# Issuing the second MLP product of a step two steps late instead of one, in a fused attention, MoE and DFT kernel

## The chip, the cores and the metric

The kernel runs as one program on one core of a Trainium2 chip. The metric is the time of one execution in device microseconds. Lower is better; the runs of one kernel are summed up by their median.

## The reference, cut to what matters

Three parts follow one another. Shapes: batch B = 4, 768 tokens, model width 384 (8 heads of 48), hidden width 1536.

```
# 1. attention with a complex decay, a recurrence over the tokens
for t in range(S):
    S = a[t] * S + k[t] v[t]^T        # a complex, S a 48 x 48 state for each head
    y[t] = q[t] @ real(S)
# 2. first MoE: tokens mixed through rank 32, then an MLP
u = x + (x^T @ U @ V)^T
x = u + relu(u @ w_ch1) @ w_ch2       # 384 -> 1536 -> 384
# 3. second MoE: 2-D Fourier transform over tokens and channels, norm, MLP
u = x + real(fft2(x))
n = (u - mean) / sqrt(var + 1e-6)
out = u + relu(n @ w_ch1) @ w_ch2
```

## The kernel before, in words

Precision. Values are kept as pairs of a high and a low part, and a product of two pairs is three matmuls (`mm3`, L89 to L93: high by high, high by low, low by high), each of 128x128 by 128x384.

The MLP, the part that the change touches. Both MoEs run through `moe_units`. The work is a row of 96 steps (b, g, f) for each MoE: batch b, half g of its tokens (384), block f of 128 hidden units out of 12. A step is

- the first product: three `mm3`, nine matmuls, into the PSUM bank `hp`;
- `hh`, the high part of relu(hp), by ScalarE (L182), and `hl`, the low part, by VectorE from `hp` and `hh` (L184); both are traced with high priority;
- the second product `second()`: nine matmuls that add the step's share to three PSUM banks `acc` (three token blocks of 128). Six of them take `hh` (L91, L92), three take `hl` (L93). At f = 11 the group (b, g) is finished: VectorE adds `acc` to `x` (L661) and SP stores it, in the second MoE to the output.

In a step the code calls the second product of the step before: the list `late` holds one step. `hp` has two PSUM banks (pool `phid`), `acc` three, everything else that needs PSUM shares three (`pms`). `hh` and `hl` have the pool's default of two buffers each.

Work beside it. While the first MoE of batch b runs, the attention of batch b+1 is traced between its steps by a `Side` object, which meters it out at an even rate: decays and their logarithms (`L`, `s`, `Th`), queries and keys (`QK`, stored and loaded again transposed as `QT`), scores `sc` with their mask `pm`, values split in two parts (`vh`, `vl`, from the loaded `vin`), the products `y` and `g` and the state `S`. Beside the last batch's first MoE and beside the second MoE it is the DFT of a batch (`f`, `ee`, `oo`, `P`, `Q`, `p_`, the normalised rows `un`). Beside the first group of the program and around the border of the two MoEs the weights are also unpacked from float64 words (`stw`, `wxw`, `w`).

Order. All of this is traced in one program order with priorities; a scheduler then gives each engine a fixed list, and an engine carries out its list in order. An instruction that has to wait holds up what stands behind it on the same engine. SP's list holds most loads and stores, and a load that waits for its buffer holds up the loads behind it. Tiles come from pools: a tile of a tag is written only when the last reader of the tile that had the buffer before is done.

Of the kernel before, what the change touches and what calls it, by code (L numbers as in the profile page):

```python
# [29 lines left out]
GSCALE = 2.0**-10  # L30
YSCALE = 2.0**-10 / FSCALE
RE_MID = 0.9
RE_LEAST = 0.72
# [8 lines left out]
def mixer_kernel(ctx, tc, a_in, qk_in, v_in, u_in, v4_in, w_in, cc_in, ss_in, cb_in, sb_in, id_in, mask_in, rows_in, out):  # L42
# [56 lines left out]
    def anchor():  # L99
        """What is kept comes after what was traced so far, on its engine."""  # L100
        for i in nc.cur_bb.bb.instructions:
            anchors[i.engine] = i
# [9 lines left out]
    def from_f64(src, name, signs=False):  # L112
        """
        Reads float64 words (as pairs of int32) and makes float32 of their bits. The high word,
        taken as a float32, is scaled by 2^-112: that takes 896 off its float64 exponent.
        """
        n = src.shape[-1]
        st = moe.tile([128, 384, 2], I32, tag="u", name=f"st{name}", bufs=5)[:, :n]
        nc.sync.dma_start(st.rearrange("p n w -> p (n w)"), src.bitcast(I32))
        low, high = st[:, :, 0], st[:, :, 1]  # L120
        x = slot(f"wx{name}")[:, :n]
        xi = x.bitcast(I32)
        kept(A.activation, x, high.bitcast(F32), AF.Abs, scale=2.0**-112)
        kept(V.tensor_scalar, low, low, 29, None, ALU.logical_shift_right)
        V.scalar_tensor_tensor(out=xi, in0=xi, scalar=3, in1=low, op0=ALU.logical_shift_left, op1=ALU.bitwise_or)  # L125
        if signs:
            A.activation(high.bitcast(F32), high.bitcast(F32), AF.Sign)
            G.tensor_tensor(x, x, high.bitcast(F32), ALU.mult)
        else:
            V.scalar_tensor_tensor(out=xi, in0=high, scalar=-(2**31), in1=xi, op0=ALU.bitwise_and, op1=ALU.bitwise_or)  # L130
        return x
# [17 lines left out]

    # ------------------------------------------------------------------ MoE  # L150
    def moe_units(mi, uT, finish, extra, batches=range(B)):
        """Hidden steps (b, g, f); the output products of a step come one step later."""
        acc = {}
# [16 lines left out]
        for b in batches:  # L170
            for g in range(2):
                for f in range(FB):
                    w = wt[mi, f]
                    hp = phid.tile([128, 512], F32, tag="hid", name=f"hp{mi}_{b}_{g}_{f}")[:, :384]
                    for k in range(3):
                        u = uT(b, g)[k]
                        ks = slice(k * 128, (k + 1) * 128)
                        mm3(hp, (w[:, 0, ks], w[:, 1, ks]), (u[:, 0], u[:, 1]), k == 0, k == 2)
                    yield b, g, f, 0
                    with tc.high_priority():  # L180
                        hh = moe.tile([128, 384], F32R, tag="hh", name=f"hh{mi}_{b}_{g}_{f}")
                        A.activation(hh, hp, AF.Relu)  # L182
                        hl = moe.tile([128, 384], F32R, tag="hl", name=f"hl{mi}_{b}_{g}_{f}")
                        V.scalar_tensor_tensor(out=hl, in0=hp, scalar=0.0, in1=f32(hh), op0=ALU.max, op1=ALU.subtract)  # L184
                    yield b, g, f, 1
                    for args in late:
                        second(*args)
                    late = [(b, g, f, hh, hl)]
        second(*late[0])

    # ------------------------------------------------------------------ attention
    BOUNDS = {
# [26 lines left out]
    def load(kind, m):  # L219
        """Decays, or queries and keys, of a pair of chunks."""  # L220
        if m >= len(PAIRS):
# [10 lines left out]
    def load_vs():  # L232
        """All values of the first batch."""
        for c0, c1 in ((0, 4), (4, NC)):
# [5 lines left out]
    def load_v(b, c):  # L240
        if c == NC:
            b, c = b + 1, 0
        if 0 < b < B:
            t = attention_pool()(f"vin{b}_{c}", "vin", 2, (128, DM))
            nc.sync.dma_start(t, v_in[b, c])
            inp["v", b, c] = t
# [6 lines left out]
    def parts(m):  # L253
        """The first pair goes chunk by chunk, so that its products start early."""
        return [slice(0, 1), slice(1, 2)] if m == 0 else [slice(0, 2)]

    def decays(m):
        """Decayed queries and keys of a pair of chunks and the tangents of its turns."""
        b, cc = PAIRS[m]
# [28 lines left out]
        def steady(js):  # L288
            """Counts re >= RE_LEAST + im^2 / 4: then |im / re| stays under 1.2."""
            re, s2_, th = of(js, a[:, 0], s2, Th)  # L290
# [4 lines left out]
        def least_re(js):  # L295
            """The same of the first batch, in two parts."""
            (re,) = of(js, a[:, 0])
            V.tensor_scalar(unread(js), re, RE_LEAST, 0.0, ALU.is_ge, ALU.add, accum_out=stat("re", b, cc[js.start]))
# [66 lines left out]
    def turns(m):  # L365
        """Rotates the queries and keys of a pair of chunks."""
        b, cc = PAIRS[m]
# [48 lines left out]
    def products(m, j):  # L416
        """Scores, outputs and the next state of one chunk."""
        b, cc = PAIRS[m]
# [44 lines left out]
        def summed(out, rows, ops):  # L463
            """Sums over the products of pairs, head by head, in plain float32 or of float16 parts."""
            for o, (l, r) in enumerate(ops):
# [73 lines left out]
        if not last:  # L539
# [13 lines left out]
            else:  # L553
# [3 lines left out]
                summed(gp, 128, [(hs(kh), vh), (hs(kh), vl), (hs(kl), vh)])  # L557
        x = xt[b, c] = xpl[0].tile([128, DM], F32, tag="x", name=f"x{n}", bufs=10)
        A.activation(x, yp, AF.Copy, scale=1.0 / FSCALE if plain else YSCALE)
# [12 lines left out]

    # ------------------------------------------------------------------ first MoE
    zst = {}
# [12 lines left out]
    def prelim(b):  # L587
        """The low-rank mixing of the tokens: z = U^T x, kept as a stack of parts."""
        zp = bank(f"z{b}", phid if b == 0 else pms)[:, :DM]
# [19 lines left out]
    def make_ut(b, g):  # L609
        """u^T = x^T + (U V part)^T of 384 tokens, as three (hi, lo) pairs."""  # L610
        uts[b, g] = pieces = []
        xs = {}

        def turn(k):
# [3 lines left out]
            if (b, g) == (0, 0):  # L618
                xs[k] = xpl[0].tile([128, DM], F32, tag="x", name=f"xs0_0_{k}", bufs=10)
            else:  # L620
# [58 lines left out]
    def urgent(gen, n=None):  # L679
        """Steps that go before what was traced up to n instructions ago."""  # L680
        while True:
# [77 lines left out]
    class Side:  # L759
        """Steps that go between the MoE's: `total` steps over `slots` slots."""  # L760

# [12 lines left out]

    # ------------------------------------------------------------------ 2-D DFT, norm, second MoE
    pfl = [None]
# [16 lines left out]
    def dft(b):  # L793
        """u = x + Re(DFT2(x)); rows 384 + j of u hold token 768 - j (j > 0) and 384 (j = 0)."""
        (cch, ccl), (ssh, ssl), (cbh, cbl), (sbh, sbl) = (fc[x] for x in ("cc", "ss", "cb", "sb"))
# [13 lines left out]
        def fold(out, x, op):  # L809
            """Columns d and 384 - d."""  # L810
            n = 193 if op == ALU.add else 192
# [48 lines left out]
        for j in range(3):  # L860
            js = slice(j * 128, (j + 1) * 128)
            pp = bank(f"P{b}_{j}")[:, :194]
            for m, w in enumerate((128, 66)):
                mm3(pp, (ach[:w, m, js], acl[:w, m, js]), (cbh[:w, m], cbl[:w, m]), m == 0, m == 1)
            p_ = ft(f"p_.{b}_{j}", [128, 194], bufs=2)
            A.copy(p_, pp)
# [37 lines left out]
    def make_un(b, g):  # L904
        """Normalised rows, transposed, as three (hi, lo) pairs."""
        mv, rs = rstd[b]
# [21 lines left out]

    # ------------------------------------------------------------------ the program
    ident = const("ident", [128, 128])  # L930
# [76 lines left out]

    # ------------------------------------------------------------------ any other decays and sizes
    def verdict():
        """1 where a bound of the chunked attention's number range was not kept, as an int32."""  # L1010
        tests = [(i, test) for i, x in enumerate(BOUNDS.values()) for test in x]
# [11 lines left out]
    def recurrence(xd):  # L1023
        """The attention token by token; partitions (b, x quarter, h), decays of any size."""
        N = 32
# [73 lines left out]
    def rest(xd):  # L1099
        """Everything after the attention, one batch at a time."""  # L1100
        with tc.For_i(0, B, 1) as bv:
# [4 lines left out]
            for c in range(NC):  # L1106
                xt[r, c] = xpl[0].tile([128, DM], F32, tag="x", name=f"xr{c}", bufs=10)
                nc.sync.dma_start(xt[r, c], xd[bass.ds(bv, 1), c].rearrange("o p m -> (o p) m"))
# [116 lines left out]
```

## Time and profile before

| | before |
|---|---|
| median of 3 runs | 1039.2 us (1037.37 to 1039.5) |
| profiled execution, its span on the core | 1035.1 us |
| TensorE matmuls busy | 885.1 us (86% of the span) |
| TensorE weight loads busy | 841.7 us (81%) |
| VectorE busy | 690.3 us (67%) |
| ScalarE busy | 441.3 us (43%) |
| GpSimd busy | 443.3 us (43%) |

The profile gives the span of the execution that it shows, from the first to the last instruction on the core; 4.1 us lie between it and the median of the runs. An engine's busy time is the time in which it carries out an instruction. Engines are named PE (TensorE's matmuls), PEld (its weight loads), DVE (VectorE), ACT (ScalarE), POOL (GpSimd) and SP (the queue that issues transfers). Seen roughly, the first 130 us are the attention of the first batch, up to about 535 us the first MoE runs beside the attention of the other batches, up to about 697 us it runs beside the DFT of the first batches, and from there on it is the second MoE.

### The profile page before, as it was taken

The numbers are of one execution on the slowest core, as the hardware profiler recorded it, in microseconds if no ns is written. First come the engines' busy times: TensorE is split into PE (matmuls) and PEld (weight loads), VectorE is DVE, ScalarE is ACT, GpSimd is POOL, SyncE is SP. The second block draws the span as 40 slices with busy tenths as digits, with TensorE's granted clock in tenths as the row PEclk, the third lists the DMA queues.
The fourth block names the chain that finished last, engine by engine and source line by source line (L and its number), as shares of the span: only waits on it lengthen the run. The fifth ranks groups of instructions, "written<-read, shape, count | busy, mean of one in ns | idle before, by whom it ended". The sixth has DMA issues, their size and how long they took to land. (4 is left out here: it accounts for less than half of the span.)

```text
span 1035.1 us, 16471 instructions
## 1 busy us (share of the span) xinstructions
PE 885.1 (86%) x6338; PEld 841.7 (81%) x6338; DVE 690.3 (67%) x1104; ACT 441.3 (43%) x841; POOL 443.3 (43%) x426
## 2 busy tenths in 40 slices
PE   0059978788778787798899999779999999999997
PEld 0048777578777787787899999779999999999997
DVE  7997988897877689788764727886535554362121
ACT  6436565657545555555643224465212211222111
POOL 4445646575464645656446307776312222020000
PEclk9999899979898898989899999889999999999999
DMA  8078646834516152614135103342101021000000
GB/s 346 0 103 165 194 81 138 166 69 109 94 45 121 49 93 69 115 48 93 33 61 200 39 1 115 108 144 77 62 16 47 2 77 46 1 23 19 7 23 27
DMA packets 47097, 83.43 MB, mean 81 GB/s; under 512 B 5600, under 2 KB 36064, under 8 KB 47008
## 3 DMA queue, kind: packets, MB, share of 16 engines
q1 hardware_dynamic: 45152, 75.96, 30.8%
q0 software_dynamic: 1856, 6.31, 1.7%
q8 instruction: 52, 0.85, 0.4%
q14 instruction: 37, 0.30, 0.1%
HBM read 53.79 MB, written 9.44 MB: 61 GB/s over the span
## 5 line engine op out<-in xcount | busy, mean ns | idle before, releaser
L184 DVE SCALAR_TENSOR_TENSOR hl<-hp,hh 128x384 fp32r<-128x384 f32 x192 | 105.4, 551 | 191.8 <-ACT hh L182 186.6
L182 ACT ACTIVATE hh<-hp 128x384 fp32r<-128x384 f32 x192 | 93.1, 488 | 270.9 <-PE hp L93 249.1
L91 PE MATMUL acc<-w,hh 128*128 128x384 f32 x576 | 202.4, 352 | 2.0 <-ACT hh L182 2.0
L93 PE MATMUL acc<-w,hl 128*128 128x384 f32 x576 | 166.1, 352 | 38.4 <-DVE hl L184 38.2
L92 PE MATMUL acc<-w,hh 128*128 128x384 f32 x576 | 197.4, 343 | 0.0
L93 PEld LDWEIGHTS acc<-w,hl 128*128 128x128 f32 x576 | 106.9, 195 | 45.4 <-DVE hl L184 45.1
L91 PEld LDWEIGHTS acc<-w,hh 128*128 128x128 f32 x576 | 111.4, 193 | 4.3 <-ACT hh L182 3.0
L92 PEld LDWEIGHTS acc<-w,hh 128*128 128x128 f32 x576 | 111.5, 194 | 0.0
L91 PE MATMUL hp<-u,w 128*128 128x384 f32 x288 | 103.0, 359 | 6.2 <-ACT w L141 3.1
L92 PE MATMUL hp<-u,w 128*128 128x384 f32 x288 | 103.7, 360 | 1.2 <-POOL u L630 1.0
L93 PE MATMUL hp<-u,w 128*128 128x384 f32 x288 | 102.4, 356 | 0.0
L92 PE MATMUL hp<-n,w 128*128 128x384 f32 x288 | 96.9, 336 | 1.6 <-DVE n L920 1.6
L91 PE MATMUL hp<-n,w 128*128 128x384 f32 x288 | 96.5, 336 | 1.1 <-ACT n L919 1.1
L93 PE MATMUL hp<-n,w 128*128 128x384 f32 x288 | 96.8, 336 | 0.0
L437 PE MATMUL sc<-QT 96*128 96x128 f32 x384 | 66.6, 328 | 11.4 <-DMA QT<-QK 10.5
L437 PEld LDWEIGHTS sc<-QT 96*128 96x128 f32 x384 | 60.7, 232 | 14.3 <-issue 11.3
L142 POOL TENSOR_TENSOR w<-wxw,w 128x384 fp32r<-128x384 f32 x48 | 58.8, 1235 | 21.9 <-ACT w L141 21.7
L451 PE MATMUL kp<-ident,QK 128*128 128x128 f32 x120 | 20.5, 297 | 53.7 <-POOL QK L409 48.6
L91 PEld LDWEIGHTS hp<-u,w 128*128 128x128 f32 x288 | 58.5, 203 | 7.0 <-ACT w L141 3.3
L451 PEld LDWEIGHTS kp<-ident,QK 128*128 128x128 f32 x120 | 16.1, 155 | 55.5 <-POOL QK L409 48.6
L92 PEld LDWEIGHTS hp<-u,w 128*128 128x128 f32 x288 | 58.6, 203 | 2.2 <-POOL u L630 1.6
L93 PEld LDWEIGHTS hp<-u,w 128*128 128x128 f32 x288 | 58.3, 203 | 0.0
(302 smaller groups left out, 2056.4 us busy)
## 6 DMA issues: line engine op xcount, KB each, us to landing
QT<-QK SPq DMA_DIRECT2D x144, 129.0 KB
stw<-in_w_dram SPq DMA_DIRECT2D x48, 384.0 KB
ain<-in_a_dram SPq DMA_DIRECT2D x12, 768.0 KB
qkin<-in_qk_dram SPq DMA_DIRECT2D x12, 768.0 KB
x1d<-x SPq DMA_DIRECT2D x24, 192.0 KB
vin<-in_v_dram SPq DMA_DIRECT2D x18, 192.0 KB
lo<-x1d SPq DMA_DIRECT2D x12, 192.0 KB
out_dram<-lo SPq DMA_DIRECT2D x12, 192.0 KB
```

Of the source, the lines that this page charges most:

```text
L91: T.matmul(o, ah, bh, start=start, stop=False, skip_group_check=skip)
L92: T.matmul(o, ah, bl, start=False, stop=False, skip_group_check=skip)
L93: T.matmul(o, al, bh, start=False, stop=stop, skip_group_check=skip)
L142: G.tensor_tensor(w[:, 1, zs], x, f32(w[:, 0, zs]), ALU.subtract)
L182: A.activation(hh, hp, AF.Relu)
L184: V.scalar_tensor_tensor(out=hl, in0=hp, scalar=0.0, in1=f32(hh), op0=ALU.max, op1=ALU.subtract)
L437: T.matmul(ps[:, h, :], q[:, 128:256], q[:, :128], start=True, stop=True)
L451: T.transpose(kp[z][:, i * 128 : (i + 1) * 128], QK[:, z, i, 128:256], ident)
```

## The change

The second product of a step is issued two steps later: the list `late` holds two steps, and only what lies deeper is issued. So `hh` and `hl` live one step longer and get three buffers each. To make room, `vin` (loaded values) goes from two buffers to one, `x` (the attention's output, input of the MoE) from ten to nine, and `p_` (a piece of the DFT) from two to one. Line numbers after the change are one to two higher.

```diff
+LATE = 2
...
                     with tc.high_priority():
-                        hh = moe.tile([128, 384], F32R, tag="hh", name=f"hh{mi}_{b}_{g}_{f}")
+                        hh = moe.tile([128, 384], F32R, tag="hh", bufs=LATE + 1, name=f"hh{mi}_{b}_{g}_{f}")
                         A.activation(hh, hp, AF.Relu)
-                        hl = moe.tile([128, 384], F32R, tag="hl", name=f"hl{mi}_{b}_{g}_{f}")
+                        hl = moe.tile([128, 384], F32R, tag="hl", bufs=LATE + 1, name=f"hl{mi}_{b}_{g}_{f}")
                         V.scalar_tensor_tensor(out=hl, in0=hp, scalar=0.0, in1=f32(hh), op0=ALU.max, op1=ALU.subtract)
                     yield b, g, f, 1
-                    for args in late:
-                        second(*args)
-                    late = [(b, g, f, hh, hl)]
-        second(*late[0])
+                    late.append((b, g, f, hh, hl))
+                    if len(late) > LATE:
+                        second(*late.pop(0))
+        for args in late:
+            second(*args)
...
-            t = attention_pool()(f"vin{b}_{c}", "vin", 2, (128, DM))
+            t = attention_pool()(f"vin{b}_{c}", "vin", 1, (128, DM))
...
-        x = xt[b, c] = xpl[0].tile([128, DM], F32, tag="x", name=f"x{n}", bufs=10)
+        x = xt[b, c] = xpl[0].tile([128, DM], F32, tag="x", name=f"x{n}", bufs=9)
...
-            p_ = ft(f"p_.{b}_{j}", [128, 194], bufs=2)
+            p_ = ft(f"p_.{b}_{j}", [128, 194], bufs=1)
```

The first place is VectorE in the first batch's second group (b = 0, g = 1), from `hl` of step 2 on. The names end in the step and a running number (`hl_0_1_3_...` is batch 0, group 1, step 3). Before:

```order
L184 SCALAR_TENSOR_TENSOR hl_0_1_2_2048<-hp_0_1_2_2008,hh_0_1_2_2046 128x384
L442 TENSOR_TENSOR pm_5_0_2286<-sc_5_0_2242,mask 128x512
L565 SCALAR_TENSOR_TENSOR S_4_2198<-g_4_2197,S_4_2198 96x384
L313 SCALAR_TENSOR_TENSOR L_2_2630<-s_2_2631,L_2_2630 128x768
L353 SCALAR_TENSOR_TENSOR s_0_2034<-Th_0_2035,s_0_2034 128x768
L501 TENSOR_TENSOR ql_5_2291<-QT_5_1893,qh_5_2290 96x1024
L381 SCALAR_TENSOR_TENSOR Th_0_2035<-one,T_0_2032 128x256 x2
L487 SCALAR_TENSOR_TENSOR vl_0_2621<-vin_0_2315,vh_0_2620 128x384
L381 SCALAR_TENSOR_TENSOR Th_0_2035<-one,T_0_2032 128x256
L184 SCALAR_TENSOR_TENSOR hl_0_1_3_2106<-hp_0_1_3_2074,hh_0_1_3_2104 128x384
L442 TENSOR_TENSOR pm_5_1_2298<-sc_5_1_2281,mask 128x512
L184 SCALAR_TENSOR_TENSOR hl_0_1_4_2232<-hp_0_1_4_2187,hh_0_1_4_2230 128x384
```

And with the change, from just behind `pm` of the same chunk on:

```order
L567 SCALAR_TENSOR_TENSOR S_4_2189<-g_4_2188,S_4_2189 96x384
L185 SCALAR_TENSOR_TENSOR hl_0_1_3_2097<-hp_0_1_3_2065,hh_0_1_3_2095 128x384
L315 SCALAR_TENSOR_TENSOR L_2_2621<-s_2_2622,L_2_2621 128x768
L355 SCALAR_TENSOR_TENSOR s_0_2022<-Th_0_2023,s_0_2022 128x768
L503 TENSOR_TENSOR ql_5_2282<-QT_5_1884,qh_5_2281 96x1024
L383 SCALAR_TENSOR_TENSOR Th_0_2023<-one,T_0_2020 128x256 x2
L489 SCALAR_TENSOR_TENSOR vl_0_2612<-vin_0_2306,vh_0_2611 128x384
L383 SCALAR_TENSOR_TENSOR Th_0_2023<-one,T_0_2020 128x256
L444 TENSOR_TENSOR pm_5_1_2289<-sc_5_1_2272,mask 128x512
L185 SCALAR_TENSOR_TENSOR hl_0_1_4_2223<-hp_0_1_4_2178,hh_0_1_4_2221 128x384
```

Seven instructions of the attention have moved from ahead of `hl` of step 3 to behind it; ahead of `hl` of step 4 stand the same ones as before.

The second place is TensorE around the same step. Before, from the second product of step 3 (the high part) to the first product of step 5; of each run of matmuls on one tile some rows stand:

```order
L92 MATMUL acc_0_1_2_1998<-w_3_860,hh_0_1_3_2104 128x384
L599 MATMUL z_2398<-xh_0_2399,ust 128x384
L600 MATMUL z_2398<-xl_0_2400,ust 128x384
L599 MATMUL z_2398<-xh_1_2405,ust 128x384
L93 MATMUL acc_0_1_0_1996<-w_3_860,hl_0_1_3_2106 128x384
L93 MATMUL acc_0_1_1_1997<-w_3_860,hl_0_1_3_2106 128x384
L93 MATMUL acc_0_1_2_1998<-w_3_860,hl_0_1_3_2106 128x384
L91 MATMUL hp_0_1_5_2271<-u_1_0_1690,w_5_954 128x384
```

With the change, from the end of the first product of step 4 on:

```order
L94 MATMUL hp_0_1_4_2178<-u_1_2_1821,w_4_934 128x384
L92 MATMUL acc_0_1_0_2053<-w_2_770,hh_0_1_2_2034 128x384
...
L94 MATMUL acc_0_1_2_2055<-w_2_770,hl_0_1_2_2036 128x384
L439 MATMUL sc_5_1_2272<-QT_5_1884 128x128 x4
L92 MATMUL hp_0_1_5_2262<-u_1_0_1681,w_5_954 128x384
...
L94 MATMUL hp_0_1_5_2262<-u_1_2_1821,w_5_954 128x384
L92 MATMUL acc_0_1_0_2053<-w_3_860,hh_0_1_3_2095 128x384
...
L94 MATMUL acc_0_1_2_2055<-w_3_860,hl_0_1_3_2097 128x384
```

Behind the first product of step 4 now stand the second product of step 2, the first of step 5 and only then the second of step 3.

The third place is VectorE at the end of the first MoE (batch 3, group 1, steps 10 and 11; `f`, `eel`, `oo` and `un` belong to the DFT of the second batch or to the second MoE's input). Before:

```order
L184 SCALAR_TENSOR_TENSOR hl_3_1_9_6742<-hp_3_1_9_6713,hh_3_1_9_6740 128x384
L812 TENSOR_TENSOR f_1_7056<-xo_1_7052 128x191
L911 TENSOR_SCALAR un_1_1_7207<-hi_1_5821,mv_6224,rs_6420 128x384
L812 TENSOR_TENSOR f_1_7056<-ye_1_7053 128x192
L814 COPY f_1_7056<-ye_1_7053 128x1
L831 TENSOR_TENSOR ee_6972<-f_1_7056 128x193 x2
L911 TENSOR_SCALAR un_1_2_7209<-hi_2_5822,mv_6224,rs_6420 128x384
L184 SCALAR_TENSOR_TENSOR hl_3_1_10_6800<-hp_3_1_10_6770,hh_3_1_10_6798 128x384
L840 TENSOR_TENSOR eel_7118<-ee_6972,eeh_7117 128x776
L812 TENSOR_TENSOR f_1_7056<-x_1_1_7050 128x191
```

With the change, from the same `hl` on:

```order
L185 SCALAR_TENSOR_TENSOR hl_3_1_9_6733<-hp_3_1_9_6704,hh_3_1_9_6731 128x384
L109 TENSOR_SCALAR stw_5_1_6641<-stw_5_1_6641 128x384
L185 SCALAR_TENSOR_TENSOR hl_3_1_10_6791<-hp_3_1_10_6761,hh_3_1_10_6789 128x384
L126 SCALAR_TENSOR_TENSOR wxw_5_1_6643<-wxw_5_1_6643,stw_5_1_6641 128x384
L109 TENSOR_SCALAR stw_6_0_6671<-stw_6_0_6671 128x384
L126 SCALAR_TENSOR_TENSOR wxw_6_0_6673<-wxw_6_0_6673,stw_6_0_6671 128x384
L814 TENSOR_TENSOR f_0_6983<-xe_0_6978 128x192
L816 COPY f_0_6983<-xe_0_6978 128x1
L814 TENSOR_TENSOR f_0_6983<-xo_0_6979 128x191
L185 SCALAR_TENSOR_TENSOR hl_3_1_11_6842<-hp_3_1_11_6819,hh_3_1_11_6840 128x384
```

The pieces `f_1`, `ee`, `un` and `eel` of the second half have moved to behind the last `hl` of the first MoE.

## Rows read from the trace of the kernel before

**Rows 1.** Page, engines: busy us (share of the span) and instructions.
```profile
PE 885.1 (86%) x6338; PEld 841.7 (81%) x6338; DVE 690.3 (67%) x1104; ACT 441.3 (43%) x841; POOL 443.3 (43%) x426
```

**Rows 2.** Busy time by stretch (start:end, length; columns in the first row).
```profile
core 0: us, PE busy (x) PEld busy (x) DVE busy (x) ACT busy (x) POOL busy (x), PEclk, DMA share, GB/s
...
240.00:535.00 295.00, 244.43 (x1983) 233.27 (x1982) 232.33 (x300) 164.43 (x303) 163.21 (x148) 0.91 0.37 74
535.00:625.00 90.00, 88.88 (x644) 87.11 (x643) 41.11 (x74) 28.17 (x61) 31.26 (x36) 1.00 0.25 84
625.00:697.00 72.00, 61.14 (x337) 57.84 (x335) 64.41 (x118) 35.74 (x76) 54.84 (x58) 0.91 0.38 117
697.00:1035.00 338.00, 331.47 (x2001) 327.54 (x1998) 142.37 (x319) 76.21 (x161) 62.26 (x79) 0.99 0.11 34
```

**Rows 3.** Page, chain that ended last, shares by engine.
```profile
PE 32%; DVE 4%; issue 1%; DMA 1%; POOL 1%; ACT 0%; DVEq 0%; SPq 0%; POOLq 0%
```

**Rows 4.** Page, costliest groups: count, busy, mean ns, idle before and what ended it.
```profile
L93 PE MATMUL acc<-w,hl 128*128 128x384 f32 x576 | 166.1, 352 | 38.4 <-DVE hl L184 38.2
```

**Rows 5.** Waits of PE from 240 to 535: us in total, times, longest.
```profile
PE acc L93 <- DVE hl L184: 26.8, 10, 6.4
PE g L469 <- DVE kl L461: 15.1, 6, 5.4
```

**Rows 6.** Waits of DVE from 240 to 535.
```profile
DVE L L326 <- POOL s L325: 16.0, 4, 7.2
DVE hl L184 <- ACT hh L182: 11.8, 10, 3.5
DVE pm L442 <- PE sc L437: 9.2, 7, 3.1
...
DVE S L565 <- PE g L469: 2.2, 2, 1.6
```

**Rows 7.** Timeline of PE: start us, us, instruction [idle before, what ended it].
```profile
260.23 0.34 PE L599 MATMUL z<-xh,ust 128*128 128x384 f32 x1
266.98 1.33 PE L93 MATMUL acc<-w,hl 128*128 128x384 f32 x3 [6.42 <-DVE hl L184]
...
394.29 0.62 PE L93 MATMUL acc<-w,hl 128*128 128x384 f32 x2 [2.72 <-DVE hl L184]
```

**Rows 8.** Timeline of DVE from 250 to 268.
```profile
250.72 0.56 DVE L184 SCALAR_TENSOR_TENSOR hl<-hp,hh 128x384 fp32r<-128x384 f32 x1 [0.43 <-ACT hh L182]
...
262.93 2.95 DVE L487 SCALAR_TENSOR_TENSOR vl<-vin,vh 128x384 f16<-128x384 f32 x1
...
266.40 0.52 DVE L184 SCALAR_TENSOR_TENSOR hl<-hp,hh 128x384 fp32r<-128x384 f32 x1
...
267.45 0.54 DVE L184 SCALAR_TENSOR_TENSOR hl<-hp,hh 128x384 fp32r<-128x384 f32 x1
```

**Rows 9.** Busy time from 260 to 270, columns as in rows 2.
```profile
260.00:270.00 10.00, 3.58 (x13) 3.26 (x12) 10.00 (x12) 1.13 (x2) 6.69 (x4) 0.67 0.07 20
```

**Rows 10.** Timeline of PE in the second MoE.
```profile
899.94 0.33 PE L91 MATMUL hp<-n,w 128*128 128x384 f32 x1
...
901.33 0.34 PE L93 MATMUL hp<-n,w 128*128 128x384 f32 x1
```

**Rows 11.** Waits of PE from 625 to 697.
```profile
PE acc L93 <- DVE hl L184: 5.7, 3, 3.6
```

**Rows 12.** Groups of DVE instructions from 649 to 697: count, busy us, mean ns, idle before.
```profile
L812 DVE TENSOR_TENSOR f<-ye 128x192 f32<-128x192 f32 x2 | 4.7, 2334 | 0.0
```

**Rows 13.** DMA issues from 240 to 535.
```profile
vin<-in_v_dram SPq DMA_DIRECT2D x10, 192.0 KB
```

**Rows 14.** Tile `vh`: idle time before its instructions, by what ended it.
```profile
  DMA vin<-in_v_dram: 3.8, 1
```

**Rows 15.** Tile `x`: its transfers, issue to landing.
```profile
DMA to landing us min/median/max: 5.2/5.2/5.2
```

More of the change, by code (lines that the diff above doesn't have):

```diff
@@ L618, in turn @@
             if (b, g) == (0, 0):
-                xs[k] = xpl[0].tile([128, DM], F32, tag="x", name=f"xs0_0_{k}", bufs=10)
+                xs[k] = xpl[0].tile([128, DM], F32, tag="x", name=f"xs0_0_{k}", bufs=9)
             else:
@@ L1106, in rest @@
             for c in range(NC):
-                xt[r, c] = xpl[0].tile([128, DM], F32, tag="x", name=f"xr{c}", bufs=10)
+                xt[r, c] = xpl[0].tile([128, DM], F32, tag="x", name=f"xr{c}", bufs=9)
                 nc.sync.dma_start(xt[r, c], xd[bass.ds(bv, 1), c].rearrange("o p m -> (o p) m"))
```

## The prediction

> **What bounds the kernel now.** I read the page first, then the busy times by stretch, then the waits of TensorE and VectorE in the longest attention stretch, then one wait instruction by instruction. TensorE is busy for 885.1 of 1035.1 us [rows 1], and the chain that ended last is mostly its matmuls [rows 3]: any gain has to come out of the time in which it stands or runs at its lower clock. The table by stretch [rows 2] says where that is. From 697 on (second MoE) TensorE is busy for 331.47 of 338.00 us at a granted clock of 0.99, from 535 to 625 for 88.88 of 90.00: together 7.7 us are idle, with nothing worth having. From 240 to 535, where the attention of the next batch runs beside the first MoE, it is busy for 244.43 of 295.00 us, so 50.6 are idle, at a clock of 0.91; from 625 to 697 (border to the second MoE) 10.9 of 72 are idle. VectorE is busy for 232.33 of the 295 and for 64.41 of the 72, so in the second case it paces the stretch.
>
> The change can act on one kind of wait: the third matmul of each triple, on `hl`, stands for 26.8 us, in ten waits, in 240 to 535 [rows 5], of 38.4 in the whole execution [rows 4]; three more cost 5.7 us in 625 to 697 [rows 11]. The next one in the list, `g<-kl` with 15.1, is attention work that the change doesn't shorten. On VectorE's side the idle time is spread: 16.0 us on GpSimd's `s`, 11.8 on ScalarE's `hh`, 9.2 and 2.2 on TensorE's `sc` and `g` [rows 6]. Only the last two items are TensorE being late.
>
> **The change, step by step.** *No instruction is added or removed*: 18 matmuls, one `hh`, one `hl` a step as before. At the undisturbed rate nine matmuls start within eight pitches from 899.94 to 901.33 [rows 10], 0.174 us each; a step of 18 costs 3.1 us, three matmuls 0.52, twelve 2.1.
>
> *What a second step of delay buys.* Take the longest wait. TensorE finishes its last covered matmul at 260.23 + 0.34 = 260.57 and stands for 6.42 us until `hl` of step 3 is there at about 266.9 [rows 7]. VectorE had finished the `hl` before it at 251.3; nine other operations came next, `vl` with 2.95 us the longest, and only at 266.40 did this `hl` start [rows 8]. The order of the changed kernel (VectorE's rows in the section on the change) puts this `hl` ahead of seven of them, which looks like the whole 6.42. But the seven now stand between it and `hl` of step 4, which is no earlier: it ran at 267.45 to 267.99 [rows 8] behind the same work. There are two PSUM banks for `hp`, so the first product of step 6 cannot start before `hl` of step 4 has read its bank. Until then TensorE has what its rows in that section show: nine matmuls of `hp` of step 5 and the three `hl` matmuls of step 3 more than before, 2.1 us. It stands from 262.7 to 268.0, resumes 1.0 us later than before and 2.1 us further on. **This place gains 1.1 us of 6.4.** The wait is handed to the next bank, not removed.
>
> *The nine others in this stretch.* In eight of them the order likewise puts the `hl` that was waited for ahead of the work that delayed it; in the ninth (first step of a group) five more operations come ahead of it. For each of the nine waits whose `hl` moves, the least is the three matmuls by which the need for `hl` moves away in the plain pattern (15 matmuls between the end of `hp` and the first use before, 18 after): 0.52 us. The place worked out gives 1.1, and the ceiling is the whole 26.8. So 4.7 to 9.9 us, and I take the middle, **-7.3**.
>
> *What is given back at the group borders.* I gave every VectorE instruction its own duration from the trace and summed what stands ahead of each `hl` in the two orders. Inside a group the sum falls by 1 to 12 us a step; at the first step of the next group it is back: -1.2, +4.1 and 0.0 us in the three borders of this stretch. Side work is put off, not saved, and VectorE has to have done it all by then. The +4.1 falls on a step at which TensorE waited already; one more step of products (3.1) covers part of it. Between 0 and +4.1 I take **+2**.
>
> *The border to the second MoE.* Here the three waits (5.7) lose their cause, but 14.8 us of VectorE work (pieces of the next DFT: `f`, `ee`, `oo`, `un`; [rows 12] has their largest group) go from ahead of the last `hl` of the first MoE to behind it, and at the first `hl` of the second MoE the sum is +1.3. VectorE idles 7.6 of the 72 us, so that it decides here. Between -1.6 (three times 0.52) and +7 (below) I take **0**. Second MoE: more slack for a wait that isn't there, 0; its cover is the 98% of TensorE's time.
>
> *Fewer buffers.* With one buffer for `vin` the load of a chunk has to wait until `vl` of the chunk before has read it, and SP's queue behind it (loads of `QT`, of the next decays) waits too. Ten loads in 295 us [rows 13] are 29 us apart, and 192 KB land in 5.2 us, as the transfers of `x` do [rows 15], so I take 0; unhidden it costs one wait like the 3.8 us that `vh` had once [rows 14]. One `x` less makes the fourth `x` of a batch wait for a store, 5.2 us at three batch borders if ScalarE stands there with `hh` behind it; hidden by the steps between, 0. `p_` is a copy of 194 columns on a stretch with a full TensorE: 0.
>
> **Sum**: -7.3 + 2 + 0 + 0 = -5.3. The profiled execution has a span of 1035.1 us, 4.1 under the median of the runs, 1039.2; 1029.8 and the same 4.1 make **1034**. 0.2%, about 2 us, is what a measurement of this kernel can tell from no change.
>
> By the Trainium skill ("Perfetto Trace Analysis", Identifying the Most-Contended Engine) TensorE's headroom is judged by the busy share of its weight loads, not of its matmuls, and VectorE's by occupancy; by that, these two are level in 240 to 535, 233.27 and 232.33 us of 295 [rows 2], and the rule would have the change gain nothing there, since it takes no work from either. The trace agrees with the level shares; it also shows VectorE idle for 62.7 us, which leaves room for a gain, so that the rule makes a rival and not the forecast.
>
> **Rivals.** *A, the forecast*: small gain at each wait, part given back; own range 1028 to 1037; 41%. *B, VectorE paces the stretch anyway*: what TensorE gains inside a group it loses standing at the next border or at `g<-kl`. For it: the sums that return to about 0, and 16.0 us on GpSimd's `s`, that no order of `hl` shortens. Against it: 11.4 us of VectorE's idle time is TensorE's lateness. No change, 1039; 27%. *C, slower, by the border to the second MoE*: 14.8 + 1.3 = 16.1 us more VectorE work stand between the last `hl` of one MoE and the first of the other, covered by one more step, 3.1; with the 5.7 of before given back that is 16.1 - 3.1 - 5.7 = +7, and with nothing won before, 1046. It decides if VectorE does not use the earlier time, that is if its idle time in this stretch grows above 7.6 us. Against it: the work ahead of that border is only 1.3 us more, so a VectorE that never idles arrives as before. 21%. *D, the waits really go*: nine waits, 26.8 - 2.7 = 24.1 us, vanish (the tenth is the one at a group's first step [rows 7]), since TensorE's earlier `sc` and `g` also pull VectorE's chain forward (the 11.4 us); with +2 that is -22, 1017. For it: the clock, whose mean over the 10 us with the longest wait was 0.67 [rows 9], between its levels of 2.4 GHz (1.0) and 1.2 GHz (0.5), stays up too. Against it: the bank of `hp`. 11%.
>
> **Numbers.** 1034 is A. The range reaches half-way into D and C, 1024 to 1043, which leaves out about 6 and 11 in 100. Faster: nearly all of A (0.39), D, and 0.04 of B, 0.54; within 0.2%: 0.19 of B, 0.02 of A and 0.03 of C, 0.24; slower 0.22.
>
> **What the changed profile would show.** Right: `acc` on `hl` almost gone from TensorE's waits, and in its place `hp` on `hl` (the bank), two thirds as long; idle time of TensorE in the attention stretch down by some 5 of 50.6 us; the second MoE as long as before. Wrong: `hp<-hl` short as well and the attention stretch 20 us shorter (D); TensorE's idle time unchanged, with more of it right behind a group's last step (B); VectorE idle above 7.6 us and TensorE's waits above 12 us around the border to the second MoE (C); or ScalarE standing at `x` or `vh` for a DMA (the buffers).

## The result and the profile after

The changed kernel takes 1053.17 us (median of 4 runs, 1050.76 to 1053.86) against 1038.86 before: a ratio of 1.0133, 95% interval 1.0113 to 1.0152. It is slower by 14 us where 5 us of gain were forecast, and lies outside the range (1024 to 1043). The profiled executions differ by 16.9 us in span (1052.0 against 1035.1); the one of the changed kernel is the slowest of its four, so part of the 16.9, which is 2.6 more than the medians differ by, is spread between executions.

The page of the changed kernel, in the order of [rows 1] and [rows 3], with the granted clock in 40 slices between them:

```profile
PE 889.1 (85%) x6338; PEld 842.3 (80%) x6338; DVE 688.4 (65%) x1104; ACT 442.6 (42%) x841; POOL 429.9 (41%) x426
...
PEclk9978998878889898899899999959999999999999
...
PE 41%; DVE 22%; DMA 7%; ACT 5%; issue 4%; POOL 2%; SPq 1%; DVEq 0%; POOLq 0%; ACTq 0%
```

The work is the same and no engine is busier than before by more than 4 us, so most of the time went into standing. The clock has a hole (5) at two thirds of the span, at the border of the two MoEs. The shares of the two chains can't be held against each other: the chain before [rows 3] is followed back only to 633 us, the new one to 180. From the last group of the first MoE on, which both cover, VectorE has 38 us in the one and 37 in the other.

To place the loss I took the start of `hh` of the same step in ScalarE's timeline of both profiles:

| step (MoE, batch, half, f) | before, us | after, us | later by |
|---|---|---|---|
| 0, 0, 1, 0 | 239.9 | 240.8 | 0.8 |
| 0, 1, 1, 0 | 388.0 | 392.4 | 4.4 |
| 0, 2, 0, 0 | 464.1 | 467.9 | 3.8 |
| 0, 2, 1, 0 | 533.7 | 541.6 | 8.0 |
| 0, 3, 1, 0 | 627.9 | 635.1 | 7.2 |
| 0, 3, 1, 11 | 678.4 | 678.9 | 0.5 |
| 1, 0, 0, 0 | 694.9 | 708.3 | 13.5 |
| 1, 0, 1, 0 | 736.6 | 750.7 | 14.1 |
| 1, 3, 1, 11 | 1025.4 | 1040.5 | 15.1 |

Two stretches lose: the attention stretch up to step (0, 3, 1, 0) 6.4 us, and the last group of the first MoE with the border behind it, up to (1, 0, 1, 0), 6.9 us. Inside the last group 6.7 us are won, and 13.0 are lost between its last step and the next group's first. The second MoE keeps its length within 1 us. The last 1.8 us to the span's end are mostly no loss: with two steps of delay one more second product, nine matmuls or 1.6 us, is left behind the last `hh`.

**The attention stretch.** TensorE's waits in the changed kernel from 240 to 560, to be held against [rows 5]:

```profile
PE hp L92 <- DVE hl L185: 16.3, 5, 7.3
PE xp L619 <- DVE pm L444: 6.7, 3, 3.2
PE g L471 <- ACT kh L462: 6.6, 1, 6.6
PE kp L453 <- DVE pm L444: 4.2, 4, 1.8
PE z L602 <- DVE xl L600: 3.9, 1, 3.9
PE kp L453 <- DVE xs L629: 3.9, 3, 2.4
PE y L471 <- DVE pm L444: 3.6, 3, 2.3
PE g L471 <- DVE kl L463: 3.2, 2, 2.2
```

The waits of `acc` on `hl` (26.8 us) left the list; `hp` now waits for `hl` (16.3), and most of the other lines are attention and token-mixing work of TensorE waiting for VectorE. Its waits on `pm`, `xs` and `xl` rose from 2.7 us to 22.3; for some 16 of these the operation waited for stands one or two `hl` further back in VectorE's list than before, for the rest, with the longest wait on `pm` (3.2), it does not. The waits of `g` on `kl` fell from 15.1 to 3.2, and one of 6.6 on ScalarE's `kh` is new. The sum did not fall. The next fences are the busy times by group (columns as in [rows 2]), before and after, each from a group's first `hh` to the next:

```profile
239.90:316.10 76.20, 58.47 (x454) 55.46 (x453) 61.12 (x79) 41.68 (x77) 41.66 (x33) 0.92 0.35 77
316.10:388.00 71.90, 61.23 (x530) 58.85 (x530) 53.42 (x71) 42.03 (x80) 38.04 (x42) 0.89 0.44 81
388.00:464.10 76.10, 62.26 (x463) 58.29 (x462) 62.53 (x81) 41.18 (x75) 44.29 (x32) 0.89 0.33 70
464.10:533.70 69.60, 61.28 (x531) 59.47 (x530) 54.13 (x72) 38.34 (x74) 38.02 (x41) 0.93 0.37 68
```

```profile
240.80:319.00 78.20, 60.38 (x406) 56.52 (x404) 58.81 (x74) 40.87 (x75) 40.32 (x31) 0.85 0.33 73
319.00:392.40 73.40, 60.42 (x582) 57.08 (x581) 58.77 (x81) 44.52 (x82) 42.77 (x46) 0.95 0.42 93
392.40:467.90 75.50, 60.74 (x408) 57.17 (x408) 58.29 (x74) 38.98 (x71) 34.19 (x28) 0.84 0.33 71
467.90:541.60 73.70, 63.68 (x568) 60.03 (x567) 53.04 (x73) 40.24 (x74) 37.90 (x44) 0.91 0.33 60
```

TensorE is busy for 243.2 of 293.8 us before and 245.2 of 300.8 after: 50.6 us idle became 55.6, and as good as the same number of matmuls (1978 and 1964 rows) took 2.0 us more. The counts by group show that whole pieces of attention moved from one group to the next (454 to 406, then 530 to 582). VectorE does not pace this stretch by its work: it is busy for 231.2 us before and 228.9 after, so its idle time rose too, from 62.6 to 71.9.

**The border to the second MoE.** TensorE's timeline in the changed kernel, where its longest new wait is:

```profile
683.07 0.69 PE L94 MATMUL acc<-w,hl 128*128 128x384 f32 x1 [2.21 <-DVE hl L185]
...
690.21 0.52 PE L93 MATMUL hp<-n,w 128*128 128x384 f32 x1
690.53 0.52 PE L94 MATMUL hp<-n,w 128*128 128x384 f32 x1
700.95 0.53 PE L92 MATMUL ac<-cc,eeh 128*128 128x194 f32 x1 [9.90 <-ACT eeh L841]
```

And what it waited for, on VectorE and on ScalarE:

```profile
694.94 1.16 DVE L814 TENSOR_TENSOR f<-xe 128x192 f32<-128x192 f32 x1
...
699.40 0.63 DVE L833 TENSOR_TENSOR ee<-f 128x193 f32<-128x193 f32 x2
```

```profile
700.06 0.84 ACT L841 CAST eeh<-ee 128x776 fp32r<-128x776 f32 x1 [3.34 <-DVE ee L833]
...
701.66 0.47 ACT L921 CAST n<-nt 128x384 fp32r<-128x384 f32 x1
```

Most of the pieces `f` and `ee` of the DFT that stood ahead of the last `hl` now run from 682.9 on, behind it. TensorE's list has the DFT's product `ac` next, which needs them (`eeh`); and the third row block `n`, which the first products of the second MoE need, stands behind `eeh` on ScalarE. So both of TensorE's jobs wait for the same late pieces. From the last `hh` of the first MoE to the first of the second (678.39 to 694.86 before, 678.86 to 708.32 after) VectorE is nearly full in both kernels, but with 15.66 us of work before and 28.68 after:

```profile
678.39:694.86 16.47, 12.18 (x66) 11.08 (x66) 15.66 (x27) 11.43 (x25) 12.00 (x13) 0.85 0.36 115
```

```profile
678.86:708.32 29.46, 15.40 (x57) 13.14 (x58) 28.68 (x48) 12.48 (x26) 21.39 (x23) 0.56 0.30 90
```

Busy time around the wait, with the change:

```profile
680.00:682.00 2.00, 0.86 (x5) 0.54 (x4) 2.00 (x4) 0.85 (x3) 2.00 (x2) 1.00 0.00 0
684.00:690.00 6.00, 4.57 (x14) 3.55 (x13) 5.85 (x13) 1.92 (x4) 3.84 (x5) 0.50 0.43 132
690.00:700.00 10.00, 1.05 (x4) 0.54 (x2) 9.89 (x19) 1.39 (x3) 7.28 (x7) 0.50 0.46 138
700.00:710.00 10.00, 9.05 (x41) 8.64 (x41) 9.48 (x15) 7.70 (x16) 5.97 (x8) 0.50 0.20 45
714.00:716.00 2.00, 2.00 (x14) 2.00 (x13) 1.65 (x4) 1.85 (x4) 0.98 (x2) 1.00 0.13 12
```

TensorE is idle and VectorE full for 10 us. The granted clock is 1.00 up to 682 and 0.50 from 684 on, TensorE's lower level of 1.2 GHz: it fell ahead of the long wait, where TensorE had been busy for 0.86 of 2.00 us and stood for 2.21 us on `hl`. It stays at 0.50 through the wait and the 10 us after it, and is back at 1.00 in 714 to 716. Two matmuls of 128x384 start 0.32 us apart there (690.21 and 690.53) and 0.174 in [rows 10]. From 680 to 716 the mean granted clock is 0.57, and 0.91 in the same stretch of the kernel before. The Trainium skill ("TensorE: Matmul & The Clock Gate", "What's actually happening") says that an idle TensorE is clocked at 1.2 GHz; the trace agrees, with 0.50 from 690 to 700, where TensorE is busy for 1.05 us.

### The profile page after: what moved, and what is told of

The parts are those of the page before. It is cut to its first block, busy times and chain, and to the rows that moved or that the text cites. A ratio compares the mean times of both kernels' runs of the same rounds, so it can differ in the third digit from the quotient of the medians.

```text
span 1052.0 us, 16462 instructions
## 1 busy us (share of the span) xinstructions
PE 889.1 (85%) x6338; PEld 842.3 (80%) x6338; DVE 688.4 (65%) x1104; ACT 442.6 (42%) x841; POOL 429.9 (41%) x426
## 4 chain that ended last, share of the span: by engine, by line
PE 41%; DVE 22%; DMA 7%; ACT 5%; issue 4%; POOL 2%; SPq 1%; DVEq 0%; POOLq 0%; ACTq 0%
PE hp L92 6%; PE hp L93 6%; PE hp L94 6%; PE acc L92 6%; PE acc L94 6%; PE acc L93 6%; DMA QT<-QK 4%; DVE L L342 3%; DVE Th L383 3%; DMA stw<-in_w_dram 1%; DVE vl L489 1%; DVE hl L185 1%; SPq L414 1%; DVE f L814 1%; DVE QK L410 1%
## 5 line engine op out<-in xcount | busy, mean ns | idle before, releaser
L94 PE MATMUL acc<-w,hl 128*128 128x384 f32 x576 | 185.9, 344 | 3.0 <-DVE hl L185 3.0
L92 PE MATMUL hp<-u,w 128*128 128x384 f32 x288 | 107.6, 378 | 26.6 <-DVE hl L185 23.4
L94 PEld LDWEIGHTS acc<-w,hl 128*128 128x128 f32 x576 | 110.6, 194 | 3.7 <-DVE hl L185 3.6
L93 PE MATMUL hp<-u,w 128*128 128x384 f32 x288 | 105.0, 365 | 2.8 <-POOL u L632 2.8
L94 PE MATMUL hp<-u,w 128*128 128x384 f32 x288 | 104.0, 362 | 0.0
L92 PEld LDWEIGHTS hp<-u,w 128*128 128x128 f32 x288 | 59.6, 209 | 30.8 <-DVE hl L185 26.8
L453 PE MATMUL kp<-ident,QK 128*128 128x128 f32 x120 | 23.0, 317 | 61.3 <-POOL QK L411 48.9
L439 PE MATMUL sc<-QT 96*128 96x128 f32 x384 | 60.5, 308 | 13.8 <-DMA QT<-QK 11.1
L439 PEld LDWEIGHTS sc<-QT 96*128 96x128 f32 x384 | 55.4, 216 | 17.0 <-issue 14.2
L143 POOL TENSOR_TENSOR w<-wxw,w 128x384 fp32r<-128x384 f32 x48 | 53.1, 1117 | 26.0 <-ACT w L142 25.9
L93 PEld LDWEIGHTS hp<-u,w 128*128 128x128 f32 x288 | 60.3, 209 | 3.7 <-POOL u L632 3.4
L94 PEld LDWEIGHTS hp<-u,w 128*128 128x128 f32 x288 | 59.8, 208 | 0.0
```

The source lines that it names most:

```text
L92: T.matmul(o, ah, bh, start=start, stop=False, skip_group_check=skip)
L93: T.matmul(o, ah, bl, start=False, stop=False, skip_group_check=skip)
L94: T.matmul(o, al, bh, start=False, stop=stop, skip_group_check=skip)
L143: G.tensor_tensor(w[:, 1, zs], x, f32(w[:, 0, zs]), ALU.subtract)
L439: T.matmul(ps[:, h, :], q[:, 128:256], q[:, :128], start=True, stop=True)
L453: T.transpose(kp[z][:, i * 128 : (i + 1) * 128], QK[:, z, i, 128:256], ident)
```

## The experiments

Twelve kernels. "Late by n" is the number of steps by which the second product follows; ratios are to the kernel before, with 95% intervals.

### Buffers and MoEs apart

**Buffers alone**: the kernel before (late by one) with the smaller numbers of buffers for `vin`, `x` and `p_`.

```diff
-            t = attention_pool()(f"vin{b}_{c}", "vin", 2, (128, DM))
+            t = attention_pool()(f"vin{b}_{c}", "vin", 1, (128, DM))
...
-        x = xt[b, c] = xpl[0].tile([128, DM], F32, tag="x", name=f"x{n}", bufs=10)
+        x = xt[b, c] = xpl[0].tile([128, DM], F32, tag="x", name=f"x{n}", bufs=9)
...
-            p_ = ft(f"p_.{b}_{j}", [128, 194], bufs=2)
+            p_ = ft(f"p_.{b}_{j}", [128, 194], bufs=1)
```

> The second product one step late as before, only the buffers of the change (vin 1, x 9, p_ 1). Theory O (order): the delay of two steps lets the fixed order put VectorE's attention and DFT work behind hl, and the time is lost at the group borders; the buffers cost nothing: 1037 to 1041 us. Theory B (buffers): loads of v and writes of x that wait hold up ScalarE and SP: 1045 to 1054.

Measured 1038.89 us, ratio 1.0018 (0.9999 to 1.0037). Theory B falls: by the interval the buffers cost between nothing and 4 us, not the 6 to 15 of theory B. The opposite corner (late by two with the old buffers) was not run.

**Late by two in one MoE only**, with all buffers of the change:

```diff
-                    if len(late) > LATE:
+                    while len(late) > (LATE if mi == 0 else 1):
```

> All buffers of the change; two steps late in the first MoE only, one step in the second. O: the whole loss lies in the first MoE and at its end, so 1051 to 1055, as the change. B: the same 1051 to 1055.

Measured 1051.98 us, 1.0172 (1.0127 to 1.0217). And with `mi == 1` in its place:

> All buffers of the change; two steps late in the second MoE only. O: as before, 1037 to 1041, since the border is entered with the old order. B: 1045 to 1054, as the buffers are small here too.

Measured 1038.26 us, 0.9992 (0.9969 to 1.0016). The whole loss belongs to the delay in the first MoE; in the second, where no wait of TensorE on `hl` shows in the kernel before, it neither costs nor gives.

### The border

**One step in the last group of the first MoE only**:

```diff
-                    if len(late) > LATE:
+                    while len(late) > (LATE if mi == 1 or b != 3 or g == 0 else 1):
```

> The change, but the last group of the first MoE (batch 3, second half) goes back to one step late. O: VectorE's order at the border to the second MoE is that of before, so the idle 9.9 us at ac and the lower clock behind it go: 1040 to 1047; what stays is the 8 us of the attention stretch. B: 1051 to 1055.

Measured 1042.78 us, 1.0047 (1.0023 to 1.0072): some 9 us of the 14 are gone. The granted clock there is 1.00 again:

```profile
690.00:700.00 10.00, 7.96 (x53) 6.95 (x53) 9.90 (x16) 6.98 (x16) 7.68 (x8) 1.00 0.53 174
```

**The delay kept, the order at the border mended**: the rows of the second MoE's first group traced urgently.

```diff
-            ut = make_ut(b, 1) if g == 0 else make_ut(b + 1, 0) if more else make_un(0, 0)
+            ut = make_ut(b, 1) if g == 0 else make_ut(b + 1, 0) if more else urgent(make_un(0, 0), 200)
```

> The change, and the normalised rows of the second MoE's first group traced urgently, which takes VectorE's DFT work back ahead of the last hl of the first MoE (net 0 us there instead of -14.8, by the durations of before) and n ahead of eeh on ScalarE. Theory O (order at the border costs 9 to 13 us): 1040 to 1046, with only the attention stretch's loss left. Rival P (it is the later product itself: the release of the weights' slots one step later, which makes the weights of the second MoE late): 1050 to 1055, since that is not touched.

Measured 1041.17 us, 1.0036 (1.0016 to 1.0055). The wait of 9.90 us at `ac` is gone from TensorE's list around the border (660 to 715):

```profile
PE hp L92 <- DVE hl L185: 4.3, 2, 2.8
PE hp L92 <- ACT n L921: 3.8, 1, 3.8
```

> Control: the same urgent rows in the kernel before. O and P: 1036 to 1041, as before, since its order at the border was already so.

That control, the same line in the kernel before, gave 1036.86 us, 1.0001 (0.9982 to 1.0020): the line itself wins nothing. So the border's loss is one of the order that the delay brings with it, not of the delayed product itself or of weights that come late; theory P falls. Which of the two moves does it, VectorE's pieces or `n` ahead of `eeh` on ScalarE, the run doesn't separate.

### The attention stretch

The next runs are built on the one with urgent rows (1041.17 us). VectorE's order is the same up to the last group of the first MoE in four kernels: the change, the delay in the first MoE only, one step in the last group, and urgent rows. At step (0, 2, 1, 0) their profiles are 2.8, 6.3, 8.0 and 9.0 us later than the profile before, and three profiles with one step of delay there (buffers alone, the delay in the second MoE only, urgent rows alone) are -2.4, -2.9 and +1.0. So the loss there is real, some 7 us in these profiles, and one profile can be off by 3; by the medians of runs it is smaller, some 4 us (1041.17 with urgent rows late by two, 1036.86 late by one). All four lose some 7 us in one place: from `hh` of step (0, 2, 0, 9) to `hh` of (0, 2, 0, 10) it takes 2.8 us in the kernel before, 9.7 to 10.1 in the four, and 5.1 with the buffers alone.

**Attention earlier**:

```diff
-                side = Side(attention(b + 1), (58, 48, 48)[b], 40)
+                side = Side(attention(b + 1), (58, 48, 48)[b], 37)
```

> The run with urgent rows, and the attention traced over 37 half steps instead of 40, so that VectorE's attention work stands where it stood before or up to 15 us earlier instead of up to 12 us later. O: the attention stretch's loss of 4 to 8 us goes too, and the later product's slack can show: 1031 to 1040. P, or a TensorE that pays for the product itself: as without the rate, 1040 to 1046.

Measured 1044.42 us, 1.0065 (1.0043 to 1.0087): not faster, and 3 us over the run with urgent rows, though the intervals overlap. Theory O in its simple form (VectorE's attention work should stand earlier) falls here; the time lies in the range of its rival, a TensorE that pays for the product itself.

**`hl` pinned behind the VectorE work traced before it**:

```diff
-                        V.scalar_tensor_tensor(out=hl, in0=hp, scalar=0.0, in1=f32(hh), op0=ALU.max, op1=ALU.subtract)
+                        pins = [i for i in nc.cur_bb.bb.instructions if i.engine == V.engine] if mi == 0 and b in (0, 1, 2) else []
+                        with tc.issue_after(pins[-1]) if pins else ExitStack():
+                            V.scalar_tensor_tensor(out=hl, in0=hp, scalar=0.0, in1=f32(hh), op0=ALU.max, op1=ALU.subtract)
```

> The run with urgent rows (late by two), and in batches 0 to 2 of the first MoE each hl is issued after the VectorE work traced before it. By the durations of before, the VectorE work ahead of hl is then within 2.5 us of the order before at most steps of the groups (in the fourth group's second neighbour, batch 2 first half, 0 to -3 instead of -9 to -12 at six of ten steps). Theory O: the attention stretch's loss of 4 to 5 us goes with the order: 1034 to 1039. Rival M (the loss is TensorE's: the second product of two steps before stands ahead of scores and products of the attention): as without the pin, 1040 to 1044.

> Control: the same pins and urgent rows, one step late. O and M: hl stands behind 0 to 6 us more VectorE work than before, with one step of cover: 1037 to 1046.

Measured 1046.69 us late by two, 1.0077 (1.0054 to 1.0100), and 1049.34 us late by one, 1.0109 (1.0079 to 1.0140). None of the three ranges holds (O, M and the control's): the pin costs more than the loss it was to mend, so that it decides nothing between O and M. TensorE's first wait from 240 to 540 in the first of them:

```profile
PE hp L92 <- DVE hl L187: 22.3, 6, 8.1
```

and in the second:

```profile
PE acc L93 <- DVE hl L186: 20.9, 8, 6.1
PE acc L91 <- ACT hh L182: 9.2, 5, 5.0
```

`hl` is late again, with either delay. Under the same pin the later product is 2.7 us faster, but the intervals overlap, so that this stays open.

**Two steps only in the middle of a group**:

```diff
-                    if len(late) > LATE:
+                    while len(late) > (LATE if mi == 1 or 1 < f < FB - 2 else 1):
```

> The run with urgent rows, two steps late only in steps 2 to 9 of a group of the first MoE, one step at its ends. O: less VectorE work put back (0 to -1 us at half of the steps in place of -2 to -12, and the longest pieces still moved): 1036 to 1041. M: 1039 to 1043.

Measured 1038.65 us, 0.9994 (0.9977 to 1.0011): the loss is gone, and nothing is won. Its profile is 12.4 us ahead of the one before at step (0, 2, 0, 0) and 1.2 us behind at (0, 2, 1, 0): a lead inside the attention stretch is not kept. Such leads are no mark of the delay: with the buffers alone the profile is 13.9 us ahead at step (0, 1, 1, 8) and 2.4 at (0, 2, 1, 0). From step (0, 2, 0, 9) to (0, 2, 0, 10) it takes 4.6 us here, in place of the 10 above. It has the delay in fewer steps as well as none at the ends of the groups, and which of the two counts is not shown. This run also takes the delay out of the ends of the last group, which the urgent rows had already mended.

**Three banks for `hp`**, two for everything else, late by two and late by one:

```diff
-    phid = ctx.enter_context(tc.tile_pool(name="phid", bufs=2, space=PSUM))
-    pms = ctx.enter_context(tc.tile_pool(name="pms", bufs=3, space=PSUM))
+    phid = ctx.enter_context(tc.tile_pool(name="phid", bufs=3, space=PSUM))
+    pms = ctx.enter_context(tc.tile_pool(name="pms", bufs=2, space=PSUM))
```

> The run with urgent rows, with three PSUM banks for hp and two for everything else (three before). By the prediction's step the waits of hp on hl, 16.3 us in the attention stretch, are waits for a bank and go, to under 5 us. O: that does not make it faster, since VectorE's attention work moves back by 10 to 20 us more: 1045 to 1065. If the bank of hp were what costs the time: 1028 to 1036.

> Control for three banks of hp and two for everything else: the same banks and urgent rows with the second product one step late. If the 27 us of the run late by two with these banks came from its order, this one, in which the VectorE work also stands 5 to 20 us further back than before, should be slow too: 1050 to 1068. If they came from the later product together with three banks: 1037 to 1045.

Measured 1065.42 us, 1.0264 (1.0224 to 1.0304), and 1063.24 us, 1.0248 (1.0226 to 1.0269). With the third bank `hp` no longer waits for `hl`; TensorE's first waits from 240 to 720, late by two:

```profile
PE zv L628 <- DVE zst L607: 8.2, 2, 5.1
PE kp L453 <- DVE pm L444: 6.7, 2, 3.8
PE z L602 <- DVE xl L600: 6.0, 5, 3.9
```

The bank was what `hp` waited for, as the prediction had it, but freeing it buys nothing: token mixing and attention wait instead, and the whole is 24 us slower. The control shows that the delay has no part in these 24 us. Whether they come from VectorE's work standing 5 to 20 us further back, or from one bank less for everything else, the two runs don't separate.

## Why the prediction was wrong

**What bounds the kernel**: right. The stretches from 535 to 625 and from 697 on kept their length, and everything happened in the other two. But the chain that "is mostly its matmuls" [rows 3] was no ground for it: its shares add up to 39% of the span, and it is followed back only to 633 us, so that it says nothing of the attention stretch.

**The worked place**: the mechanism was right, the name of the next waiter wrong, and the forecast gain of 1.1 us did not come. The changed kernel's VectorE there, against [rows 8]:

```profile
258.37 0.54 DVE L185 SCALAR_TENSOR_TENSOR hl<-hp,hh 128x384 fp32r<-128x384 f32 x1
258.83 1.36 DVE L315 SCALAR_TENSOR_TENSOR L<-s,L 128x768 f32<-128x768 f32 x1
...
270.05 0.54 DVE L185 SCALAR_TENSOR_TENSOR hl<-hp,hh 128x384 fp32r<-128x384 f32 x1
```

and TensorE, against [rows 7]:

```profile
266.67 0.34 PE L93 MATMUL acc<-w,hh 128*128 128x384 f32 x1
270.18 0.90 PE L619 MATMUL xp<-ident,x 128*128 128x128 f32 x3 [3.18 <-DVE pm L444]
270.74 0.67 PE L92 MATMUL hp<-u,w 128*128 128x384 f32 x1
```

`hl` of step 3 comes 8.0 us earlier, as the order said, and `hl` of step 4 at 270.05 behind the same work, as forecast. TensorE does resume later (270.18 in place of 266.98), with 18 matmuls of the MLP (3.1 us) more behind it: nothing is won. And it stands at a transpose `xp` that waits for `pm`, an attention operation in the same VectorE burst, not at `hp`: by the code `xp` and the scores that `pm` reads share the three banks of `pms`. I had followed only the MLP's own chain and its bank.

**"So 4.7 to 9.9 us, and I take the middle, -7.3"** is the step that failed in the attention stretch, in its sign. It added up nine waits as if each gain stayed, and put at nothing what TensorE's attention and token mixing would wait for in the new order. The sign for `hp` on `hl` came as forecast (16.3 us of 26.8, nearly two thirds), but TensorE's idle time rose by 5.0 us where it was to fall by some 5. The runs show that a gain inside a group isn't kept (12.4 us ahead and 1.2 behind one group later, in the run with the delay in mid-group), and that attention work on VectorE is waited for in place of `hl`: 22.3 us on `pm`, `xs` and `xl` in the list above, where it was 2.7. The wait `g<-kl`, which the prediction said the change doesn't shorten, fell by 11.9 us, and even so nothing was won. The term **+2** for the group borders was too small, whether or not the borders are the place: the stretch as a whole lost 6.4 us. I had shown myself that the sums come back to 0 at each border, and should have given rival B more weight.

**"Between -1.6 and +7 I take 0"** is the step that failed at the border to the second MoE. The last group with its border lost 6.9 us, the price that rival C had worked out (+7), and its signs of recognition appeared. From step (0, 3, 1, 0) to the first of the second MoE, before and after:

```profile
627.90:694.86 66.96, 56.10 (x304) 52.91 (x303) 60.69 (x111) 32.54 (x69) 50.80 (x54) 0.91 0.40 122
```

```profile
635.10:708.32 73.22, 57.95 (x306) 54.36 (x305) 61.67 (x113) 34.42 (x72) 53.68 (x57) 0.82 0.40 119
```

VectorE's idle time grew from 6.3 to 11.5 us, above the 7.6 named, and the waits that end TensorE's idle time there sum to 15.2 us, above the 12 named. The parts of C's price came out as well: 6.7 us won inside the last group (C had 5.7) and 13.0 lost behind it (16.1 - 3.1). C was right on place and price and wrong on the waiter, which is not `hl` but `ac` and `n` behind the DFT's pieces. How much of the 6.9 us the lower clock adds, which C left out, is not shown. That VectorE "arrives as before" failed because it did not work through: over these steps it waits longer for the weights' words, before and after:

```profile
DVE stw L108 <- DMA stw<-in_w_dram: 2.1, 2, 1.6
```

```profile
DVE stw L109 <- DMA stw<-in_w_dram: 5.2, 7, 1.8
```

A later release of the weights' slots (their last reader comes one step later) does not explain it alone: with urgent rows, late by two as well, this wait is 1.7 us over the same steps. In the changed order `stw` stands ahead of the DFT's pieces, so that VectorE comes to it earlier; whether that is the reason was not tried apart.

**Fewer buffers**: 0 lies in the interval (1.0018, 0.9999 to 1.0037). **Second MoE**: right, 0. **Rivals**: C came true at the border (7 us). B was right that the attention stretch gives nothing, but it has no loss in it, and 6 us were lost there in the profile; its ground, that VectorE paces the stretch, is not borne out, since VectorE's idle time grew by 9.3 us. D did not happen anywhere.

What stays open is why the attention stretch lost 6 us rather than nothing. The loss was gone when only steps 2 to 9 of a group were late by two. Tracing the attention earlier, or pinning `hl` behind VectorE's earlier work, did not take it away, so that it is not simply a matter of what stands first on VectorE. Rival M, that the later second product stands ahead of TensorE's own attention work, is not excluded by any run.

## What to carry to other kernels

A deeper delay changes the whole fixed order, not just the wait it is aimed at: list what moves behind the freed operation on the in-order engine, and follow each moved operation to its own reader, not only the chain that is freed. Where work is only put off, it is due at the next place where a group or a stage must be complete; a lead won before that place was worth nothing here, and at the border of the two MoEs the clock was low on top of the wait (0.57 from 680 to 716, 0.91 before). If a delay is to be tried, try it by stage first: here it was worth nothing in one MoE and harmful in the other, where the loss was gone with one step at the ends of the groups. And before two chains that ended last are compared, see how far back each was followed.

## What the runs showed of the hardware that was not expected

The same VectorE instruction varies far more than its mean says: `vl` (128x384) takes 0.52 to 5.99 us within the changed kernel's profile, with a median of 0.64. The profiles of the four kernels with one VectorE order differ by up to 6 us at the same step of the attention stretch (2.8 to 9.0 us late). Others agree far more closely: the kernel before and its control with urgent rows, whose VectorE order is the same up to the last group of the first MoE, keep an offset of 1.0 to 1.3 us at every first step of a group from (0, 1, 0, 0) to (0, 3, 1, 0). From step (1, 0, 1, 0) to (1, 3, 1, 11) the second MoE repeats within 1 us of the kernel before, but for the two runs with three banks for `hp`, which are 2.9 and 3.9 us shorter.
